# Spreading a tile's row stores over the next tile, and reordering the matmuls, in the backward chain of a recurrent-memory attention block

## The chip, the cores and the metric

The kernel runs on one core of one Trainium2 chip. The metric is device time in microseconds (us) of one execution. Times are medians of several executions; profiles are of one execution each. Runs of one kernel lie 15 to 50 us apart, so where a few microseconds matter I compare stretches inside a trace and not totals.

## The reference

The reference computes a forward pass and all its gradients: layer norm, attention with a recurrent memory, layer norm, a gated FFN. Cut to what matters:

```python
for s in range(n_seg):                       # 64 segments of 32 tokens, one after the other
    h = concat([mem, x[:, 32*s:32*s+32]])    # 8 memory rows + 32 tokens = 40 rows of 448
    q, k, v = h @ Wq, h @ Wk, h @ Wv         # 16 heads of 256
    p = softmax(mask(q @ k.T / 16))
    o = (p @ v) @ Wo
    mem = o[:, :8]                           # goes into the next segment
```

The backward pass runs through the 64 segments in the opposite order. The gradient of `mem` couples each segment to the one before it, so this part cannot be made parallel. I call it the backward chain. A token tile is 128 tokens, that is four segments. `r` is the number of a segment in its tile. The chain runs through r = 3, 2, 1, 0, and the tile's rows are stored when r = 0 is done.

## The kernel before

Forward chain, FFN and weight-gradient tail do not change. In the backward chain, each segment makes row gradients of V, K and Q heads in `blk` (32 token columns per segment) and `lo` (8 memory columns). `blk` and `lo` are stored to HBM once per tile, and the tail reads them. Q, K and V of the forward pass come back by transposing DMA loads in `load_seg`. `k.ps1()` takes one of five PSUM tiles. `k.evac(..., "v")` copies on VectorE (DVE), `"s"` on ScalarE (ACT). `nc.gpsimd.dma_start` is issued by POOL (POOLq in the views) and goes into the software DMA queue (q0 software_dynamic in the profile, 238.56 MB in the whole trace), `nc.sync` is issued by SP (SPq) into a hardware queue (q1 hardware_dynamic, 359.15 MB). `k.prio.crit()` gives the chain priority; the `px` part is filler that the scheduler fits into gaps.

```python
    WoT_sb = W(0, KC, HD)
    WkT_sb, Q_sb = W(32, MC, D), W(60, 16, P)
    WvT_sb, K_sb = W(64, MC, D), W(92, 16, P)
    WqT_sb = W(96, MC, D)
    blk = {nm: A(8 * i, 32, P) for i, nm in enumerate("kqv")}
    lo_b = {nm: [A(24 + 4 * i + 2 * e, 32, 32) for e in range(2)] for i, nm in enumerate("kqv")}
    dxT_b = [A(36 + 2 * e, 1024).bitcast(FP32).rearrange("p (c n) -> p c n", n=P) for e in range(2)]
    om2 = A(40, 1024).bitcast(FP32)
    vT = A(48, 32, 64)
    dO_sb = A(52, 16, P)
    doT = A(56, 32, 64)
    do_roll = A(60, KC, NWIN, L)
    woT_tmp = A(40, HD)
    dhx = A(62.5, KC, P)
    dmr = A(63.5, KC, 16, M)
    P_bd, dS_bd, dST_bd = [B(1.25 * i, 8, 2, L) for i in range(3)]
    Pb = [B(3.75 + 0.625 * i, 8, L) for i in range(2)]
    # ... (cut: prep_tile)
    def load_seg(s):
        nc.sync.dma_start_transpose(out=vT.rearrange("p (a b) n -> p a (b n)", b=2), in_=dr["VG"][s])
        nc.sync.dma_start_transpose(out=Q_sb, in_=dr["QT"][s])
        nc.sync.dma_start_transpose(out=K_sb, in_=dr["KT"][s])
        P_sb = Pb[s % 2]
        nc.gpsimd.dma_start(out=P_sb.rearrange("p h n -> p (h n)"), in_=dr["P_all"][s])
        for g in range(2):
            nc.gpsimd.tensor_copy(out=P_bd[64 * g:64 * g + L, :, g, :], in_=P_sb[64 * g:64 * g + L, :, :])
    # ... (cut: weight loads; then, for segment s from 63 down to 0, t, r = divmod(s, 4):)
            pss = [k.ps1() for _ in range(4)]
            for j in range(MC):
                c = cj(j)
                b, jj = divmod(j, 8)
                for kc in range(KC):
                    nc.tensor.matmul(pss[b][:, jj * L:(jj + 1) * L], lhsT=WoT_sb[:, kc, c * P:(c + 1) * P],
                                     rhs=do_roll[:, kc, sl, :], start=(kc == 0), stop=(kc == KC - 1))
            # ... (cut: evacuation to doT)
            def token_major(hf):
                ph = k.ps1()[:].bitcast(BF16)
                for i in range(8):
                    c0 = 2 * (8 * hf + i)
                    nc.tensor.transpose(ph[:, i * P:(i + 1) * P], doT[:, c0:c0 + 2, :].rearrange("p c n -> p (c n)"), ident[:, :])
                nc.scalar.copy(out=dO_sb[:, 8 * hf:8 * hf + 8, :], in_=ph.rearrange("p (c n) -> p c n", n=P))
            token_major(0)
            pD = k.ps1()
            for h in range(8):
                for g in range(2):
                    for dc in range(DC):
                        j = 2 * (2 * h + dc) + g
                        nc.tensor.matmul(pD[64 * g:64 * g + 64, h * L:(h + 1) * L], lhsT=doT[:, j, :], rhs=vT[:, j, 0:L],
                                         start=(dc == 0), stop=(dc == DC - 1), skip_group_check=True)
            token_major(1)
            # ... (cut: four DVE instructions: prod, rsum, prod, dS_bd)
            pH = k.po1()
            for wi, (nm, lhs, rhs, WT) in enumerate((("v", dO_sb, P_bd, WvT_sb), ("k", Q_sb, dS_bd, WkT_sb),
                                                     ("q", K_sb, dST_bd, WqT_sb))):
                if nm == "k":
                    pT = k.ps1()
                    for h in range(8):
                        for g in range(2):
                            nc.tensor.matmul(pT[64 * g:64 * g + L, h * L:(h + 1) * L], lhsT=dS_bd[:, h, g, :],
                                             rhs=ident[:, 64 * g:64 * g + L], start=True, stop=True, skip_group_check=True)
                    for g in range(2):
                        k.evac(dST_bd[64 * g:64 * g + L, :, g, :],
                               pT[64 * g:64 * g + L, 0:8 * L].rearrange("p (h n) -> p h n", n=L), "vs"[g])
                pp = [k.ps1() for _ in range(3)]
                head_mm(pp, lhs, rhs)
                for b in range(3):
                    c0, n, v = c12(pp[b], b)
                    k.evac(blk[nm][:, c0:c0 + n, r * SEG:(r + 1) * SEG], v[:, :, M:L], "vsv"[b])
                for b in range(3):
                    c0, n, v = c12(pp[b], b)
                    k.evac(lo[nm][:, c0:c0 + n, r * M:(r + 1) * M], v[:, :, 0:M], "svs"[b])
                for j in range(MC):
                    nc.tensor.matmul(pH[32 * (j % 4):32 * (j % 4) + 32, 0:D], lhsT=blk[nm][:, j, r * SEG:(r + 1) * SEG],
                                     rhs=WT[:, cj(j), :], start=(wi == 0 and j < 4), stop=(wi == 2 and j >= MC - 4),
                                     skip_group_check=True)
            nc.vector.tensor_copy(out=om[:, 0:224], in_=pH[:, 0:224])
            nc.scalar.copy(out=om[:, 224:D], in_=pH[:, 224:D])
            # ... (cut: pm = om x sel on TensorE, memory rows of the gradient into do_roll for segment s-1)
            nc.scalar.copy(out=dxT[:, :, r * SEG + M:(r + 1) * SEG], in_=pm3[:, :, 0:24])
        # ... (cut)
        if r == 0:
            for nm in "kqv":
                nc.gpsimd.dma_start(out=dr["X_" + nm][t], in_=blk[nm].rearrange("p c n -> p (c n)"))
                nc.gpsimd.dma_start(out=dr["M_" + nm][t], in_=lo[nm].rearrange("p c n -> p (c n)"))
            px = k.fx1()
            for wi, (nm, WT) in enumerate((("k", WkT_sb), ("q", WqT_sb), ("v", WvT_sb))):
                for j in range(MC):
                    nc.tensor.matmul(px[32 * (j % 4):32 * (j % 4) + 32, 0:D], lhsT=lo[nm][:, j, :], rhs=WT[:, cj(j), :],
                                     start=(wi == 0 and j < 4), stop=(wi == 2 and j >= MC - 4), skip_group_check=True)
            nc.scalar.copy(out=om2[:, 0:D], in_=px[:, 0:D])
            pl = k.fx1()
            for kc in range(KC):
                nc.tensor.matmul(pl[:, kc * 32:(kc + 1) * 32], lhsT=om2[:, kc * P:(kc + 1) * P], rhs=sel[:],
                                 start=True, stop=True)
            nc.scalar.copy(out=dxT.rearrange("p c (r n) -> p c r n", n=SEG)[:, :, :, 0:M],
                           in_=pl[:, 0:KC * 32].rearrange("p (c r m) -> p c r m", c=KC, m=M))
            pX = k.fx1()
            for kc in range(KC):
                nc.tensor.transpose(pX[:, kc * P:(kc + 1) * P], dxT[:, kc, :], k.identf[:, :])
            dxn = k.f32("f3", D, "dxn_sb")
            nc.scalar.copy(out=dxn[:], in_=pX[:, 0:D])
            nc.gpsimd.dma_start(out=dr["DXN"][t * P:(t + 1) * P, :], in_=dxn[:])
```

Of the kernel before, what the change touches and what calls it, by code (L numbers as in the profile page):

```python
# [9 lines left out]
FP32 = mybir.dt.float32  # L10
# [5 lines left out]
P = 128  # L16
# [130 lines left out]
def run_all(k: _K):  # L147
# [18 lines left out]
    k.B = _Arena(arena, "arB", 8.25)  # L166
# [59 lines left out]
def cj(j):  # L226
    return (j % 2) * 16 + j // 2
# [418 lines left out]
def backward_chain(k: _K):  # L646
# [13 lines left out]
    blk = {nm: A(8 * i, 32, P) for i, nm in enumerate("kqv")}  # L660
    lo_b = {nm: [A(24 + 4 * i + 2 * e, 32, 32) for e in range(2)] for i, nm in enumerate("kqv")}
    dxT_b = [A(36 + 2 * e, 1024).bitcast(FP32).rearrange("p (c n) -> p c n", n=P) for e in range(2)]
    om2 = A(40, 1024).bitcast(FP32)
# [4 lines left out]
    woT_tmp = A(40, HD)  # L668
# [13 lines left out]
# [4 lines that stand above are left out]
        P_sb = Pb[s % 2]  # L686
        nc.gpsimd.dma_start(out=P_sb.rearrange("p h n -> p (h n)"), in_=dr["P_all"][s])
        for g in range(2):
            nc.gpsimd.tensor_copy(out=P_bd[64 * g:64 * g + L, :, g, :], in_=P_sb[64 * g:64 * g + L, :, :])
# [5 lines left out]
    nc.gpsimd.memset(do_roll[:, :, (NSEG - 1) % NWIN, SEG:L], 0.0)  # L695
    om = k.f32("f1", DP, "omb")
    nc.gpsimd.memset(om[:], 0.0)
    nc.gpsimd.memset(om2[:, D:DP], 0.0)
# [15 lines left out]
    for s in range(NSEG - 1, -1, -1):  # L714
# [3 lines left out]
        lo = {nm: lo_b[nm][t % 2] for nm in "kqv"}  # L718
        dxT = dxT_b[t % 2]
# [6 lines left out]
        with k.prio.crit():  # L726
# [16 lines left out]
            token_major(0)  # L743
            pD = k.ps1()
# [6 lines left out]
            token_major(1)  # L751
# [9 lines left out]
            for wi, (nm, lhs, rhs, WT) in enumerate((("v", dO_sb, P_bd, WvT_sb), ("k", Q_sb, dS_bd, WkT_sb),  # L761
                                                     ("q", K_sb, dST_bd, WqT_sb))):
                if nm == "k":
                    pT = k.ps1()
                    for h in range(8):
                        for g in range(2):
                            nc.tensor.matmul(pT[64 * g:64 * g + L, h * L:(h + 1) * L], lhsT=dS_bd[:, h, g, :],
                                             rhs=ident[:, 64 * g:64 * g + L], start=True, stop=True, skip_group_check=True)
                    for g in range(2):
                        k.evac(dST_bd[64 * g:64 * g + L, :, g, :],  # L770
                               pT[64 * g:64 * g + L, 0:8 * L].rearrange("p (h n) -> p h n", n=L), "vs"[g])
                pp = [k.ps1() for _ in range(3)]
                head_mm(pp, lhs, rhs)
                for b in range(3):
                    c0, n, v = c12(pp[b], b)
                    k.evac(blk[nm][:, c0:c0 + n, r * SEG:(r + 1) * SEG], v[:, :, M:L], "vsv"[b])
                for b in range(3):
                    c0, n, v = c12(pp[b], b)
                    k.evac(lo[nm][:, c0:c0 + n, r * M:(r + 1) * M], v[:, :, 0:M], "svs"[b])
                for j in range(MC):  # L780
                    nc.tensor.matmul(pH[32 * (j % 4):32 * (j % 4) + 32, 0:D], lhsT=blk[nm][:, j, r * SEG:(r + 1) * SEG],  # L781
                                     rhs=WT[:, cj(j), :], start=(wi == 0 and j < 4), stop=(wi == 2 and j >= MC - 4),
                                     skip_group_check=True)
            nc.vector.tensor_copy(out=om[:, 0:224], in_=pH[:, 0:224])
# [15 lines left out]
        nc.gpsimd.tensor_copy(out=dmr[:, :, jm, :], in_=do_roll[:, :, sl, SEG:L])  # L800
# [4 lines left out]
        if r == 0:  # L805
            for nm in "kqv":
                nc.gpsimd.dma_start(out=dr["X_" + nm][t], in_=blk[nm].rearrange("p c n -> p (c n)"))
                nc.gpsimd.dma_start(out=dr["M_" + nm][t], in_=lo[nm].rearrange("p c n -> p (c n)"))
            px = k.fx1()
            for wi, (nm, WT) in enumerate((("k", WkT_sb), ("q", WqT_sb), ("v", WvT_sb))):  # L810
                for j in range(MC):
                    nc.tensor.matmul(px[32 * (j % 4):32 * (j % 4) + 32, 0:D], lhsT=lo[nm][:, j, :], rhs=WT[:, cj(j), :],  # L812
                                     start=(wi == 0 and j < 4), stop=(wi == 2 and j >= MC - 4), skip_group_check=True)
            nc.scalar.copy(out=om2[:, 0:D], in_=px[:, 0:D])
            pl = k.fx1()
            for kc in range(KC):
                nc.tensor.matmul(pl[:, kc * 32:(kc + 1) * 32], lhsT=om2[:, kc * P:(kc + 1) * P], rhs=sel[:],
                                 start=True, stop=True)
            nc.scalar.copy(out=dxT.rearrange("p c (r n) -> p c r n", n=SEG)[:, :, :, 0:M],
                           in_=pl[:, 0:KC * 32].rearrange("p (c r m) -> p c r m", c=KC, m=M))  # L820
# [5 lines left out]
            nc.gpsimd.dma_start(out=dr["DXN"][t * P:(t + 1) * P, :], in_=dxn[:])  # L826

# [205 lines left out]
```

## Time and profile before

| | |
|---|---|
| median time | 3827.32 us (3823.0 to 3843.95, 3 runs) |
| profiled run | 3806.6 us span |
| backward chain, first segment to last row matmul | 1765.9 to 2967.7 us: 1201.8 us |
| segment length, mean over tiles after the first: r = 3, 2, 1, 0 | 24.31, 16.74, 16.20, 16.62 us |
| shortest and longest r = 3 segment | 19.4 and 33.0 us |

A segment's length is the distance between the first of its 128 output-gradient matmuls (line 732, 128x40) and the first of the next segment's, from the timeline. Segment r = 3 is the first one after a tile's stores were issued. I call it the after-store segment.

The first view is one window over the chain without its first tile. It gives the busy time of each engine with the instructions counted, then the granted TensorE clock, the mean busy share of the 16 DMA engines, and GB/s:

```profile
core 0: us, PE busy (x) PEld busy (x) DVE busy (x) ACT busy (x) POOL busy (x), PEclk, DMA share, GB/s
1862.70:2954.10 1091.40, 943.73 (x21894) 670.66 (x21894) 427.93 (x1062) 390.28 (x990) 164.38 (x389) 0.95 0.79 151
```

TensorE is busy 86% of the time and DMA 79%, so both matter. The second view is the chain of waits, around the start of an after-store segment (start, us, what):

```profile
2316.57 0.48 PE fx L812 x5
2317.05 1.51 PE po L781 x32
2318.57 0.56 PE fx L812 x11
2319.13 0.36 PE psf L788 x2
2319.49 0.02 PE fx L812
2319.51 18.44 DMA arW<-KT
2337.95 0.05 issue
2338.00 0.75 PE psf L711 x16
```

The chain jumps from the Q-head matmuls at 2338.00 back to the DMA that loaded `KT`, and 18.44 us are put down to it. The third view is the DMA issues of the same window (what, issuing queue, how many, KB, median us from issue to landing):

```profile
X_v<-arA POOLq DMA_DIRECT2D x14, 1024.0 KB, 5.9
X_k<-arA POOLq DMA_DIRECT2D x14, 1024.0 KB, 15.5
X_q<-arA POOLq DMA_DIRECT2D x14, 1024.0 KB, 16.0
M_q<-arA POOLq DMA_DIRECT2D x14, 256.0 KB, 16.1
```

X_v, issued first, lands after 5.9 us. X_k and X_q, issued after it, land after 15.5 and 16.0 us.

### The profile page before, as it was taken

How to read it: one execution, taken by the hardware profiler on the slowest of the kernel's cores; microseconds unless marked ns; L12 is line 12 of the kernel's file. 1: busy time of each engine (PE TensorE's matmuls, PEld its weight loads, DVE VectorE, ACT ScalarE, POOL GpSimd, SP SyncE). 2: the span in 40 equal slices, each digit the busy share in tenths (PEclk: the TensorE clock that was granted, in tenths of full speed). 3: DMA queues.
4: the chain of work that ended last, by engine and by line, in shares of the span. 5: the costliest groups of instructions: out<-in, count | busy, mean ns of one | idle time of the engine just before them, and what ended most of it. 6: DMA issues, size and time to landing. Idle time of an engine off the chain costs nothing.

```text
span 3806.6 us, 122548 instructions
## 1 busy us (share of the span) xinstructions
PE 3141.8 (83%) x55484; PEld 2052.6 (54%) x55550; DVE 1350.1 (35%) x2969; ACT 960.6 (25%) x2181; POOL 522.8 (14%) x1129
## 2 busy tenths in 40 slices
PE   3888899888898838892888888889898667888999
PEld 2666666566666625661655656656666333333444
DVE  3443344343343326672333334434443232101101
ACT  1222222222222212330333333333333101111200
POOL 3111111111111111111111111211111111000000
PEclk9999999999998869996999989999999789999999
DMA  7544644545544497789787977787877997777552
GB/s 248 169 155 138 178 148 149 162 148 166 159 149 137 132 192 189 187 198 229 146 135 140 173 128 146 174 143 148 183 142 138 329 193 173 155 154 163 156 191 68
DMA packets 1021838, 629.13 MB, mean 165 GB/s; under 512 B 910148, under 2 KB 940660, under 8 KB 1013572
## 3 DMA queue, kind: packets, MB, share of 16 engines
q1 hardware_dynamic: 934980, 359.15, 46.0%
q0 software_dynamic: 58976, 238.56, 18.4%
q10 hardware_dynamic: 27360, 23.58, 2.2%
q8 instruction: 435, 7.13, 0.8%
q14 instruction: 87, 0.71, 0.1%
HBM read 124.49 MB, written 270.64 MB: 104 GB/s over the span
## 4 chain that ended last, share of the span: by engine, by line
PE 65%; DMA 14%; issue 7%; DVE 5%; SPq 4%; ACT 4%; POOL 1%; ACTq 0%; DVEq 0%; POOLq 0%
PE psf L382 11%; PE po L781 8%; PE psf L905 8%; PE psf L732 5%; PE po L466 4%; DMA arA<-arA 3%; PE psf L711 3%; PE psf L569 2%; PE fx L812 2%; PE psf L423 2%; PE fx L495 2%; PE fx L910 2%; PE fx L363 2%; PE psf L741 2%; PE psf L788 2%
## 5 line engine op out<-in xcount | busy, mean ns | idle before, releaser
L75 DVE CAST arA<-psf 128x320 bf16<-128x320 f32 (+6 forms) x1093 | 500.2, 479 | 1056.3 <-PE psf L905 347.0
L77 ACT CAST arA<-psf 128x480 bf16<-128x480 f32 (+6 forms) x1139 | 440.8, 407 | 1530.5 <-PE psf L382 340.6
L382 PEld LDWEIGHTS <-arW 128*128 128x128 bf16 x16384 | 435.2, 97 | 32.4 <-issue 20.3
L382 PE MATMUL psf<-arA,arW 128*128 128x40 bf16 x16384 | 437.3, 182 | 17.9 <-issue 11.4
L781 PE MATMUL po<-arW,arA 128*32 128x448 bf16 x6144 | 334.2, 360 | 42.5 <-DMA arW<-in_A_Wv_dram 21.2
L732 PE MATMUL psf<-arA,arW 128*128 128x40 bf16 x8192 | 225.7, 182 | 90.2 <-POOL arA L680 39.3
L732 PEld LDWEIGHTS <-arW 128*128 128x128 bf16 x8192 | 223.2, 98 | 107.1 <-issue 102.2
L905 PE MATMUL psf<-arW,arA 128*128 128x512 bf16 x990 | 260.8, 393 | 12.7 <-ACT arA L77 12.7
L905 PEld LDWEIGHTS <-arA 128*128 128x128 bf16 x1440 | 138.7, 100 | 213.6 <-issue 73.4
L781 PEld LDWEIGHTS <-arA 128*32 128x32 bf16 x6144 | 149.2, 97 | 176.4 <-DVE arA L75 44.1
L569 PE MATMUL psf<-arA,arW 128*128 128x256 bf16 x1344 | 166.0, 285 | 72.9 <-DMA arA<-arA 41.1
L569 PEld LDWEIGHTS <-arW 128*128 128x128 bf16 x1344 | 137.2, 102 | 103.8 <-issue 78.4
L75 DVE CAST arB<-psf 40x320 bf16<-40x320 f32 (+2 forms) x256 | 92.4, 361 | 224.8 <-PE psf L457 156.4
L363 PE MATMUL fx<-arW,arA 128*128 128x512 bf16 x456 | 121.7, 388 | 57.9 <-DMA arW<-in_A_Wv_dram 38.6
L926 PE MATMUL psf<-arW 128*128 128x448 bf16 x450 | 105.5, 388 | 62.8 <-DVE arA L75 51.5
L466 PE MATMUL po<-arW,arB 128*8 128x448 bf16 x2048 | 148.1, 445 | 2.9 <-ACT sd L86 0.4
L423 PE MATMUL psf<-arW,arB 128*32 128x512 bf16 x2048 | 149.7, 383 | 0.8 <-issue 0.7
L742 ACT COPY arA<-psf 128x1024 bf16<-128x1024 bf16 x128 | 129.5, 1012 | 55.6 <-PE psf L741 54.0
L457 PE MATMUL psf<-arB,arA 128*128 128x80 bf16 x1024 | 57.9, 221 | 97.3 <-DMA arA<-arA 77.5
L926 PEld LDWEIGHTS <-arW 128*128 128x128 bf16 x606 | 62.5, 104 | 130.2 <-issue 69.4
L812 PE MATMUL fx<-arW,arA 128*32 128x448 bf16 x1536 | 121.8, 368 | 1.5 <-issue 1.5
L495 PE MATMUL fx<-arW,arA 128*128 128x448 bf16 x512 | 120.7, 362 | 0.0
(358 smaller groups left out, 3888.5 us busy)
## 6 DMA issues: line engine op xcount, KB each, us to landing
QT<-arA POOLq DMA_DIRECT2D x64, 512.0 KB, 4.0
KT<-arA SPq DMA_DIRECT2D x64, 512.0 KB
VG<-arA SPq DMA_DIRECT2D x64, 512.0 KB
X_o<-arA POOLq DMA_DIRECT2D x40, 512.0 KB, 4.7
Vx<-arA POOLq DMA_DIRECT2D x32, 512.0 KB, 3.2
arA<-Vx SPq DMA_DIRECT2D x128, 128.0 KB
X_v<-arA POOLq DMA_DIRECT2D x16, 1024.0 KB, 5.9
X_k<-arA POOLq DMA_DIRECT2D x16, 1024.0 KB, 15.5
```

Of the source, the lines that this page charges most:

```text
L75: nc.vector.tensor_copy(out=out, in_=in_)
L77: nc.scalar.copy(out=out, in_=in_)
L363: nc.tensor.matmul(pv[:, 0:512], lhsT=hx_b[t % 2][:, kc, :], rhs=Wv_sb[:, kc, n * 512:(n + 1) * 512], start=(kc == 0), stop=(kc == KC - 1))
L382: nc.tensor.matmul(pss[b][:, jj * L:(jj + 1) * L], lhsT=W_sb[:, kc, c * P:(c + 1) * P], rhs=hT_roll[:, kc, sl, :], start=(kc == 0), stop=( ...
L423: nc.tensor.matmul(pV[b][32 * j:32 * j + 32, 0:512], lhsT=memT_pad[:, kc, :], rhs=Wv_sb[:, kc, n * 512:(n + 1) * 512], start=(kc == 0), st ...
L466: nc.tensor.matmul(pO[32 * (j % 4):32 * (j % 4) + M, 0:D], lhsT=o8[:, j, :], rhs=Wo_sb[:, cj(j), :], start=(j < 4), stop=(j >= MC - 4), sk ...
L495: nc.tensor.matmul(px[:, 0:D], lhsT=xblk[:, j, :], rhs=Wo_sb[:, cj(j), :], start=(j == 0), stop=(j == MC - 1))
L569: nc.tensor.matmul(ps[:, f2 * 256:(f2 + 1) * 256], lhsT=Wt[:, kc, c * P:(c + 1) * P], rhs=xT[:, kc, :], start=(kc == 0), stop=(kc == KC - 1))
L732: nc.tensor.matmul(pss[b][:, jj * L:(jj + 1) * L], lhsT=WoT_sb[:, kc, c * P:(c + 1) * P], rhs=do_roll[:, kc, sl, :], start=(kc == 0), stop ...
L781: nc.tensor.matmul(pH[32 * (j % 4):32 * (j % 4) + 32, 0:D], lhsT=blk[nm][:, j, r * SEG:(r + 1) * SEG], rhs=WT[:, cj(j), :], start=(wi == 0 ...
L812: nc.tensor.matmul(px[32 * (j % 4):32 * (j % 4) + 32, 0:D], lhsT=lo[nm][:, j, :], rhs=WT[:, cj(j), :], start=(wi == 0 and j < 4), stop=(wi ...
L905: nc.tensor.matmul(pa[2 * kc + g][:, 0:w], lhsT=lhs_of(b)[:, kc * P:(kc + 1) * P], rhs=rhs_of(b, g), start=(b == 0), stop=(b == nblk - 1), ...
```

## The change

The intent is threefold. The six stores of a tile (3.75 MB) become nine pieces that are issued over the whole next tile. For that, five row buffers rotate where each of V, K and Q had its own, and `dxT` and the memory columns of Q lose their second buffer to make room. Both transposes of the output gradient come before the score gradients. And the Q-head products are issued inside the K row pass, with the dS transposes after the K heads, so that TensorE has row matmuls to do while other engines evacuate.

```diff
-    blk = {nm: A(8 * i, 32, P) for i, nm in enumerate("kqv")}
-    lo_b = {nm: [A(24 + 4 * i + 2 * e, 32, 32) for e in range(2)] for i, nm in enumerate("kqv")}
-    dxT_b = [A(36 + 2 * e, 1024).bitcast(FP32).rearrange("p (c n) -> p c n", n=P) for e in range(2)]
-    om2 = A(40, 1024).bitcast(FP32)
+    blk_b = [A(8 * i, 32, P) for i in range(5)]
+    lo_b = {"v": [A(40, 32, 32), A(42, 32, 32)], "k": [A(44, 32, 32), A(46, 32, 32)], "q": [B(5, 32, 32)]}
+    dxT = B(7, 1024).bitcast(FP32).rearrange("p (c n) -> p c n", n=P)
     vT = A(48, 32, 64)
     dO_sb = A(52, 16, P)
     doT = A(56, 32, 64)
     do_roll = A(60, KC, NWIN, L)
-    woT_tmp = A(40, HD)
+    woT_tmp = A(24, HD)
 ...
-            nc.gpsimd.tensor_copy(out=P_bd[64 * g:64 * g + L, :, g, :], in_=P_sb[64 * g:64 * g + L, :, :])
+            pool_op = nc.gpsimd.tensor_copy(out=P_bd[64 * g:64 * g + L, :, g, :], in_=P_sb[64 * g:64 * g + L, :, :])
+        stores("mid", s, pool_op.ins)
+
+    pending = {}
+
+    def later(seg, place, fn):
+        pending.setdefault((place, seg), []).append(fn)
+
+    def stores(place, seg, ins):
+
+        for fn in pending.pop((place, seg), []):
+            with tc.issue_after(ins):
+                fn()
 ...
-        lo = {nm: lo_b[nm][t % 2] for nm in "kqv"}
-        dxT = dxT_b[t % 2]
+        tb = NT - 1 - t
+        lo = {nm: lo_b[nm][tb % len(lo_b[nm])] for nm in "kqv"}
+        blk = {nm: blk_b[(3 * tb + i) % 5] for i, nm in enumerate("vkq")}
 ...
             token_major(0)
+            token_major(1)
             pD = k.ps1()
 ...
+            heads("v", dO_sb, P_bd)
+            rows_in("v", WvT_sb, 0, MC)
+            heads("k", Q_sb, dS_bd)
+            pT = k.ps1()
+            for h in range(8):
+                for g in range(2):
+                    nc.tensor.matmul(pT[64 * g:64 * g + L, h * L:(h + 1) * L], lhsT=dS_bd[:, h, g, :],
+                                     rhs=ident[:, 64 * g:64 * g + L], start=True, stop=True, skip_group_check=True)
+            for g in range(2):
+                k.evac(dST_bd[64 * g:64 * g + L, :, g, :],
+                       pT[64 * g:64 * g + L, 0:8 * L].rearrange("p (h n) -> p h n", n=L), "vs"[g])
+            rows_in("k", WkT_sb, 0, 20)
+            heads("q", K_sb, dST_bd)
+            rows_in("k", WkT_sb, 20, MC)
+            rows_in("q", WqT_sb, 0, MC)
 ...
-        nc.gpsimd.tensor_copy(out=dmr[:, :, jm, :], in_=do_roll[:, :, sl, SEG:L])
+        pool_op = nc.gpsimd.tensor_copy(out=dmr[:, :, jm, :], in_=do_roll[:, :, sl, SEG:L])
+        stores("start", s, pool_op.ins)
 ...
-            for nm in "kqv":
-                nc.gpsimd.dma_start(out=dr["X_" + nm][t], in_=blk[nm].rearrange("p c n -> p (c n)"))
+            def store_x(nm, hf, t=t, blk=blk):
+                nc.gpsimd.dma_start(out=dr["X_" + nm][t][:, hf * 2048:(hf + 1) * 2048],
+                                    in_=blk[nm][:, 16 * hf:16 * hf + 16, :].rearrange("p c n -> p (c n)"))
+
+            def store_m(nm, t=t, lo=lo):
                 nc.gpsimd.dma_start(out=dr["M_" + nm][t], in_=lo[nm].rearrange("p c n -> p (c n)"))
+            due = [(lambda: store_x("v", 0), None), (lambda: store_x("v", 1), None), (lambda: store_m("q"), None),
+                   (lambda: store_m("v"), (1, "start")), (lambda: store_m("k"), (1, "start")),
+                   (lambda: store_x("k", 0), (2, "start")), (lambda: store_x("k", 1), (3, "mid")),
+                   (lambda: store_x("q", 0), (3, "start")), (lambda: store_x("q", 1), (4, "mid"))]
+            for fn, at in due:
+                if at is None or s == 0:
+                    fn()
+                else:
+                    later(s - at[0], at[1], fn)
             px = k.fx1()
-            for wi, (nm, WT) in enumerate((("k", WkT_sb), ("q", WqT_sb), ("v", WvT_sb))):
+            for wi, (nm, WT) in enumerate((("q", WqT_sb), ("k", WkT_sb), ("v", WvT_sb))):
 ...
```

In `due`, `None` means at once, and `(n, place)` means in the iteration of the n-th following segment. In the trace the `mid` pieces go out one segment earlier, because the loads that they are tied to run ahead: both halves of X_k leave in the second segment, both of X_q in the third. `tc.issue_after` fixed only their place in POOL's order here.

More of the change, by code (lines that the diff above doesn't have):

```diff
@@ L165, in run_all @@
     k.A = _Arena(arena, "arA", 65)
-    k.B = _Arena(arena, "arB", 8.25)
+    k.B = _Arena(arena, "arB", 9.25)
     k.ps1 = lambda: psum.tile([P, 512], FP32, tag="ps", name="psf", bufs=5)
@@ L695, in backward_chain @@
     nc.gpsimd.memset(do_roll[:, :, (NSEG - 1) % NWIN, SEG:L], 0.0)
+    nc.gpsimd.memset(dxT[:, KC - 1, :], 0.0)
     om = k.f32("f1", DP, "omb")
     nc.gpsimd.memset(om[:], 0.0)
-    nc.gpsimd.memset(om2[:, D:DP], 0.0)
     prep_tile(NT - 1)
@@ L750, in backward_chain @@
                                          start=(dc == 0), stop=(dc == DC - 1), skip_group_check=True)
-            token_major(1)
             pD3 = pD[:, 0:8 * L].rearrange("p (h n) -> p h n", n=L)
@@ L760, in backward_chain @@
             pH = k.po1()
-            for wi, (nm, lhs, rhs, WT) in enumerate((("v", dO_sb, P_bd, WvT_sb), ("k", Q_sb, dS_bd, WkT_sb),
-                                                     ("q", K_sb, dST_bd, WqT_sb))):
-                if nm == "k":
-                    pT = k.ps1()
-                    for h in range(8):
-                        for g in range(2):
-                            nc.tensor.matmul(pT[64 * g:64 * g + L, h * L:(h + 1) * L], lhsT=dS_bd[:, h, g, :],
-                                             rhs=ident[:, 64 * g:64 * g + L], start=True, stop=True, skip_group_check=True)
-                    for g in range(2):
-                        k.evac(dST_bd[64 * g:64 * g + L, :, g, :],
-                               pT[64 * g:64 * g + L, 0:8 * L].rearrange("p (h n) -> p h n", n=L), "vs"[g])
-                pp = [k.ps1() for _ in range(3)]
-                head_mm(pp, lhs, rhs)
+            pps = {}
@@ L774, in backward_chain, with heads @@
+            def heads(nm, lhs, rhs):
+                pps[nm] = [k.ps1() for _ in range(3)]
+                head_mm(pps[nm], lhs, rhs)
                 for b in range(3):
-                    c0, n, v = c12(pp[b], b)
+                    c0, n, v = c12(pps[nm][b], b)
                     k.evac(blk[nm][:, c0:c0 + n, r * SEG:(r + 1) * SEG], v[:, :, M:L], "vsv"[b])
                 for b in range(3):
-                    c0, n, v = c12(pp[b], b)
+                    c0, n, v = c12(pps[nm][b], b)
@@ L779, in backward_chain, with rows_in @@
                     k.evac(lo[nm][:, c0:c0 + n, r * M:(r + 1) * M], v[:, :, 0:M], "svs"[b])
-                for j in range(MC):
+            def rows_in(nm, WT, j0, j1):
+                for j in range(j0, j1):
                     nc.tensor.matmul(pH[32 * (j % 4):32 * (j % 4) + 32, 0:D], lhsT=blk[nm][:, j, r * SEG:(r + 1) * SEG],
-                                     rhs=WT[:, cj(j), :], start=(wi == 0 and j < 4), stop=(wi == 2 and j >= MC - 4),
+                                     rhs=WT[:, cj(j), :], start=(nm == "v" and j < 4), stop=(nm == "q" and j >= MC - 4),
@@ L813, in backward_chain @@
                                      start=(wi == 0 and j < 4), stop=(wi == 2 and j >= MC - 4), skip_group_check=True)
-            nc.scalar.copy(out=om2[:, 0:D], in_=px[:, 0:D])
+            om2 = k.f32("f3", D, "om2")
+            nc.scalar.copy(out=om2[:], in_=px[:, 0:D])
             pl = k.fx1()
             for kc in range(KC):
-                nc.tensor.matmul(pl[:, kc * 32:(kc + 1) * 32], lhsT=om2[:, kc * P:(kc + 1) * P], rhs=sel[:],
+                m = min(P, D - kc * P)
+                nc.tensor.matmul(pl[0:m, kc * 32:(kc + 1) * 32], lhsT=om2[:, kc * P:kc * P + m], rhs=sel[:],
                                  start=True, stop=True)
-            nc.scalar.copy(out=dxT.rearrange("p c (r n) -> p c r n", n=SEG)[:, :, :, 0:M],
-                           in_=pl[:, 0:KC * 32].rearrange("p (c r m) -> p c r m", c=KC, m=M))
+            dx4 = dxT.rearrange("p c (r n) -> p c r n", n=SEG)
+            pl4 = pl[:, 0:KC * 32].rearrange("p (c r m) -> p c r m", c=KC, m=M)
+            nc.scalar.copy(out=dx4[:, 0:3, :, 0:M], in_=pl4[:, 0:3])
+            nc.scalar.copy(out=dx4[0:64, 3, :, 0:M], in_=pl4[0:64, 3])
             pX = k.fx1()
@@ L826, in backward_chain @@
             nc.gpsimd.dma_start(out=dr["DXN"][t * P:(t + 1) * P, :], in_=dxn[:])
+    assert not pending
 def tail_phase(k: _K):
```

## The prediction

> **What bounds the kernel now.** The change touches only the backward chain: about 1766 us (first output-gradient matmul, timeline) to 2974 us of a 3806.6 us span, a recurrence over 64 segments, four to a token tile. By segment starts in the timeline, three of a tile's four segments take 16.0 to 17.2 us, nearly all TensorE chain: the chain of waits from 2359.9 shows 3.35 + 0.45 + 0.62 + 0.57 us of matmuls, 1.16 us waiting for two 1.02 us ACT copies, V rows 1.63, a 1.0 us bubble around the dS transposes, K rows 1.70, a 0.6 us bubble, Q rows 1.73, then 2.04 us to the next segment. The fourth, after a tile's row stores, takes 19.4 to 33.0 us, mean 24.3 over fifteen tiles. The chain shows why: "DMA arW<-KT 18.44" at 2319.5. Six stores (3.75 MB) are issued within 6 us, X_k and X_q land after 15.5 and 16.0 us (DMA view), and issuing that KT transpose takes 12.33 us against 2.81 in a quiet segment. [...]
>
> **What the change does.**
> 1. The same bytes go out in nine pieces over the next tile (about 1.25, 0.5, 1 and 1 MB per segment). DMA records outside the burst give roughly 9 us of transposes and 3.5 us of stores per 16 us: below saturation. Each transpose has some 10 us of slack. I expect the after-store segment to fall from 24.3 to about 16.3 us, fifteen times. Critical.
> 2. Both transposes before the scores: the second ACT copy follows the first directly (-0.15 us), but the dS chain on DVE starts 0.55 us later and, with its new order, ends about 0.7 us later; K heads then wait some 0.3 us.
> 3. Q heads inside K rows, dS transposes after K heads: the 1.0 and 0.6 us bubbles go. Sum of 2 and 3, by hand from these durations: 16.0 to about 15.7 us per segment. Small.
> 4. Cost: dxT is single now, so in the built ACT order the dxT copies of the first two segments come after the third's filler work; their two PSUM tiles stay held, leaving 3 of 5 there, and the built PE order breaks up that segment's V and K heads: estimate 17.4 us. Filler (96 matmuls of 53 ns per tile) has smaller gaps to hide in.
> 5. Start: the last Wo piece moves before the 23 us Wq transpose in the SP order: 0 to -8 us.
>
> Tile estimate: 16.3 + 16.1 + 17.4 + 16.1 + 1 residual DMA wait = 66.9 us against 73.9. Fifteen times 7 = 105 us; start -3. Predicted **3720 us**, 8 in 10 between **3685** and **3762**. Chances: faster by over 2% **0.80**, within **0.19**, slower **0.01**.
>
> **What would show it.** 1: every fourth segment within 1.5 us of the others; the KT/QT wait gone from the chain; X_k, X_q landing in under 8 us. 2, 3: row matmuls wait less on DVE, K heads wait on dS, plain segments 15.5 to 15.9 us. 4: a tile's third segment longest, its dxT copies in a bunch. Forward, FFN and weight-gradient tail unchanged within 10 us.
>
> **What would make it wrong.** Store halves colliding with transposes in every segment; the PSUM hold costing 3 us or more per tile; a lower granted clock in the denser stage; the tail waiting longer for last stores.

A tile of 66.9 us against 73.9, fifteen times 7 us, and 3 us for the start, off the 3827.32 us of the kernel before, make the 3720 us. Two of its inputs, from the trace of the kernel before: in the plain segment from 2359.9 to 2376 us the packets of the hardware queue took 8.4 us (a mean of 16 engines), in the one before it 12.2 us. The `VG`, `QT` and `KT` transposes that were issued from 2347.6 on landed 9.3, 11.3 and 11.1 us before their first matmul. "Below saturation" is an estimate from such numbers.

## The result, and the profile after

| | before | after |
|---|---|---|
| median of the runs at that time | 3825.16 us (3800.02 to 3843.95, 4 runs) | 3676.86 us (3671.49 to 3693.75, 4 runs) |
| profiled run | 3806.6 us | 3670.7 us |
| chain, first segment to last row matmul | 1201.8 us | 1076.9 us |
| segments r = 3, 2, 1, 0 | 24.31, 16.74, 16.20, 16.62 us | 16.74, 16.05, 17.11, 15.98 us |

The ratio of times is 0.9624, with a 95% interval of 0.9559 to 0.9689. A ratio is the mean time of one kernel's fast runs over that of the other's of the same rounds, so it is not quite the ratio of the medians quoted. The forecast of a gain over 2% held. The size did not: 3676.86 us is 8 us below the stated range.

The window over the chain without its first tile, changed kernel:

```profile
core 0: us, PE busy (x) PEld busy (x) DVE busy (x) ACT busy (x) POOL busy (x), PEclk, DMA share, GB/s
1845.10:2817.40 972.30, 930.88 (x21899) 664.47 (x21896) 424.38 (x1062) 385.96 (x1005) 188.24 (x436) 1.00 0.79 170
```

The same matmuls fit into 972.30 us instead of 1091.40, and TensorE is busy 96% of it. The clock rose too, from 0.95 to 1.00; that comes back below.

The chain of waits of the changed kernel, in an after-store segment from its first matmul on (line 744 is the old 732):

```profile
2636.32 3.30 PE psf L744 x128
2639.63 0.97 PE psf L753 x16
2640.60 0.62 PE psf L762 x32
2641.22 0.02 issue
2641.24 0.46 PE psf L722 x8
2641.70 0.49 PE fx L846 x8
2642.19 0.42 PE psf L722 x8
2642.61 1.63 PE po L787 x32
2644.24 0.19 PE fx L846 x4
```

No DMA stands in it. The stores of the changed kernel, in the DMA view:

```profile
X_k<-arA POOLq DMA_DIRECT2D x30, 512.0 KB, 4.0
X_q<-arA POOLq DMA_DIRECT2D x30, 512.0 KB, 3.9
X_v<-arA POOLq DMA_DIRECT2D x28, 512.0 KB, 6.2
M_q<-arB POOLq DMA_DIRECT2D x14, 256.0 KB, 5.5
```

All of this looks like the prediction. But two more views do not fit its reason, the late Q and K transposes. The first is what TensorE's matmuls waited for in the same window of the kernel before (engine, line, what ended the wait: us in total, times, longest):

```profile
PE psf L732 <- issue: 39.2, 8, 12.7
PE psf L749 <- issue: 25.8, 3, 11.6
PE psf L711 <- ACT arA L742: 21.3, 31, 1.0
PE po L781 <- DVE arA L75: 15.0, 44, 0.4
PE psf L741 <- issue: 8.8, 3, 4.6
PE psf L788 <- DVE omb L784: 7.5, 15, 0.5
PE psf L711 <- DMA arW<-QT: 5.7, 2, 4.1
PE psf L711 <- issue: 5.3, 3, 3.2
PE po L781 <- issue: 4.3, 4, 1.9
PE psf L711 <- DMA arW<-KT: 3.9, 2, 3.1
```

The two transposes cost TensorE 5.7 + 3.9 = 9.6 us in all fifteen tiles. The after-store segments are (24.31 - 16.74) x 15 = 114 us too long. The large waits are called "issue", which means that the profile shows nothing that was waited for. The timeline of the kernel before shows how such a wait looks (start, us, engine, line, what, count, idle before and what ended it):

```profile
2241.29 2.84 PE L732 MATMUL psf<-arA,arW 128*128 128x40 bf16 x93 [1.39 <-issue]
2243.97 1.02 PE L741 MATMUL psf<-ident,arA 128*128 128x128 bf16 x8
2244.92 0.94 PE L749 MATMUL psf<-arA 128*64 128x40 bf16 x27
2257.37 0.35 PE L749 MATMUL psf<-arA 128*64 128x40 bf16 x5 [11.52 <-issue]
2257.66 1.03 PE L741 MATMUL psf<-ident,arA 128*128 128x128 bf16 x8
```

TensorE stops for 11.52 us after 27 of 32 like matmuls. The other five read the same two tiles and write the same one, so there is no new data that they could have waited for. I counted TensorE's records (weight loads, matmuls and the semaphore records of its sequencer) from the start of the trace: the pauses at 2241 and 2257 lie 256 records apart, and most others a multiple of 256. Without the semaphore records no more than two of the 24 pauses counted below share a residue modulo 256.

The profile has a DMA queue of the kind "instruction", q8, and all 435 of its packets in the trace are of 16,384 bytes. In the DMA view of the kernel before (window 1862 to 2954; packets, MB, share of 16 engines):

```profile
q8 instruction: 171, 2.80, 1.1%
```

From the first after-store segment to the last row matmul 174 of these packets began, and there are 174 places where the count passes the same residue modulo 256. Of 24 pauses over 1.1 us (from the start of one record to the start of the next), 19 lie exactly there. As many blocks are fetched as TensorE passes such places. So I have a new theory, F: q8 fetches TensorE's instructions, one block for 256 of them, the burst of stores delays these fetches, and TensorE stops for want of instructions. The old one, that late transposes stop it, I call T.

The same list for the changed kernel:

```profile
PE psf L722 <- ACT arA L754: 6.3, 14, 0.5
PE fx L861 <- ACT arB L857: 4.9, 15, 0.3
PE psf L722 <- DVE arB L771: 4.3, 14, 0.3
PE psf L744 <- DVE arA L813: 3.9, 14, 0.3
PE psf L722 <- issue: 3.1, 3, 1.1
PE psf L753 <- issue: 2.8, 1, 2.8
```

Its waits for "issue" are a few microseconds.

### The profile page after: what moved, and what is told of

Read it like the earlier page. It is cut to its first block, busy times and chain, and to the rows that moved or that the text cites. A ratio compares the mean times of both kernels' runs of the same rounds, so it can differ in the third digit from the quotient of the medians.

```text
span 3670.7 us, 122624 instructions
## 1 busy us (share of the span) xinstructions
PE 3122.9 (85%) x55484; PEld 2044.1 (56%) x55550; DVE 1349.2 (37%) x2969; ACT 955.4 (26%) x2197; POOL 547.1 (15%) x1177
## 4 chain that ended last, share of the span: by engine, by line
PE 66%; DMA 12%; DVE 7%; issue 6%; SPq 4%; ACT 4%; POOL 1%; ACTq 0%; DVEq 0%; POOLq 0%
PE psf L382 12%; PE psf L944 8%; PE po L787 6%; PE psf L744 6%; PE po L466 4%; PE psf L722 3%; DMA arA<-arA 3%; PE psf L423 2%; PE fx L846 2%; PE psf L569 2%; PE fx L495 2%; PE fx L949 2%; PE fx L363 2%; PE psf L809 2%; DVE arA L75 2%
## 5 line engine op out<-in xcount | busy, mean ns | idle before, releaser
L75 DVE CAST arA<-psf 128x384 bf16<-128x384 f32 (+6 forms) x1029 | 491.9, 495 | 1002.4 <-PE psf L944 351.2
L77 ACT CAST arA<-psf 128x384 bf16<-128x384 f32 (+6 forms) x1011 | 412.0, 429 | 1475.5 <-PE psf L382 337.1
L382 PEld LDWEIGHTS <-arW 128*128 128x128 bf16 x16384 | 435.4, 98 | 28.9 <-issue 16.8
L382 PE MATMUL psf<-arA,arW 128*128 128x40 bf16 x16384 | 437.5, 182 | 14.6 <-issue 8.0
L787 PE MATMUL po<-arW,arA 128*32 128x448 bf16 x6144 | 346.7, 355 | 21.1 <-DMA arW<-in_A_Wv_dram 21.1
L744 PE MATMUL psf<-arA,arW 128*128 128x40 bf16 x8192 | 217.9, 180 | 46.0 <-POOL arA L679 40.1
L744 PEld LDWEIGHTS <-arW 128*128 128x128 bf16 x8192 | 214.0, 96 | 65.4 <-issue 64.9
L569 PEld LDWEIGHTS <-arW 128*128 128x128 bf16 x1344 | 135.9, 101 | 102.6 <-issue 79.0
L75 DVE CAST arB<-psf 40x320 bf16<-40x320 f32 x320 | 107.4, 336 | 165.1 <-PE psf L457 145.8
L77 ACT CAST arB<-psf 128x96 bf16<-128x96 f32 (+1 forms) x320 | 98.2, 307 | 200.1 <-PE psf L457 100.2
L965 PEld LDWEIGHTS <-arW 128*128 128x128 bf16 x606 | 61.8, 102 | 122.2 <-issue 72.4
L722 PEld LDWEIGHTS <-arW 128*128 128x128 bf16 x2048 | 86.9, 100 | 64.7 <-issue 61.3
```

The source lines that it names most:

```text
L75: nc.vector.tensor_copy(out=out, in_=in_)
L77: nc.scalar.copy(out=out, in_=in_)
L382: nc.tensor.matmul(pss[b][:, jj * L:(jj + 1) * L], lhsT=W_sb[:, kc, c * P:(c + 1) * P], rhs=hT_roll[:, kc, sl, :], start=(kc == 0), stop=( ...
L569: nc.tensor.matmul(ps[:, f2 * 256:(f2 + 1) * 256], lhsT=Wt[:, kc, c * P:(c + 1) * P], rhs=xT[:, kc, :], start=(kc == 0), stop=(kc == KC - 1))
L722: nc.tensor.matmul(ps[b][:, i * 2 * L:(i + 1) * 2 * L], lhsT=lhs[:, cl, :], rhs=rhs_bd[:, cl // 2, :, :].rearrange("p g n -> p (g n)"), st ...
L965: nc.tensor.matmul(pa[i][:, 0:D], lhsT=lhs_of(b, i), rhs=rhs_of(b), start=(b == 0), stop=(b == nblk - 1))
```

## The experiments

The table gives all kernels. "Chain" runs from the first segment to the last row matmul; segment means leave out the first tile; "fetch stalls" are pauses over 0.5 us of TensorE at the block boundary, after the first tile, counted from the packed traces as above (no view prints them), with their number and sum. The kernel before had medians of 3814.83, 3825.15 and 3826.10 us (e1 to e4; e5 to e9; e10 to e13).

| kernel | median us | chain | r = 3 | r = 2 | r = 1 | r = 0 | fetch stalls |
|---|---|---|---|---|---|---|---|
| before | 3825.16 | 1201.8 | 24.31 | 16.74 | 16.20 | 16.62 | 22, 89.9 us |
| e4_before_again | 3829.15 | 1205.7 | 24.60 | 16.76 | 16.14 | 16.71 | 20, 82.5 us |
| after | 3676.86 | 1076.9 | 16.74 | 16.05 | 17.11 | 15.98 | 10, 12.1 us |
| e13_after_again | 3693.09 | 1077.6 | 16.96 | 16.05 | 17.01 | 16.01 | 9, 11.5 us |
| e1_burst | 3775.48 | 1165.9 | 22.66 | 16.08 | 16.90 | 15.99 | 24, 64.6 us |
| e2_order_only | 3777.40 | 1178.1 | 23.56 | 16.05 | 16.42 | 16.30 | 22, 79.9 us |
| e3_stores_only | 3704.57 | 1096.4 | 16.79 | 16.97 | 16.78 | 16.56 | 5, 5.0 us |
| e5_k_at_once | 3792.94 | 1195.1 | 24.63 | 16.07 | 16.93 | 15.98 | 21, 95.3 us |
| e6_scores_first | 3680.38 | 1070.8 | 16.73 | 15.96 | 16.85 | 15.89 | 8, 10.2 us |
| e8_two_dxT | 3682.97 | 1080.9 | 17.28 | 16.06 | 16.54 | 16.21 | 12, 17.6 us |
| e9_dST_first | 3696.02 | 1077.7 | 17.10 | 15.88 | 17.12 | 15.82 | 9, 15.6 us |
| e10_unread (wrong results) | 3874.69 | 1227.8 | 25.41 | 17.17 | 16.29 | 16.78 | 22, 67.3 us |
| e11_act_queue | 3877.73 | 1268.6 | 25.96 | 16.24 | 16.38 | 19.75 | 23, 108.2 us |
| e12_three_fixes | 3662.14 | 1060.3 | 16.86 | 15.81 | 16.42 | 15.82 | 11, 16.6 us |

### e1_burst: all stores at once, everything else as changed

```diff
-                if at is None or s == 0:
+                if True:
```

> The changed kernel with one condition changed: all nine row stores are issued at the end of the tile again, in one burst; five buffers and the new matmul order stay. Theory A (the burst of 3.75 MB delays the Q and K transposes): the after-store segment returns from 16.7 to 20-28 us, other segments stay at 16.0-17.1, total near 3785 us (3760-3810). Rival B (what cost time was that the next tile's evacuations waited for single row buffers to be stored): five buffers cure it whatever the burst, total stays at 3677 +-12 us, after-store segment below 17.5 us.

Measured: 3775.48 us, after-store segment 22.66 us, the others unchanged. Theory A holds as to the burst, and rival B falls as the main cause: with five rotating buffers and the burst, 89 of the 125 us of the chain are lost again (1165.9 against 1076.9). What the buffers and the other parts of the change bring without spreading shows as the 12 us between e2 and this run (1178.1 to 1165.9, one trace each). Which of its effects the burst works through, this run does not say; its stalls lie at the block boundaries like those of the kernel before.

### e2_order_only: the new matmul order alone

```diff
             token_major(0)
+            token_major(1)
             pD = k.ps1()
 ...
-            for wi, (nm, lhs, rhs, WT) in enumerate((("v", dO_sb, P_bd, WvT_sb), ...
+            heads("v", dO_sb, P_bd)
+            rows_in("v", WvT_sb, 0, MC)
+            heads("k", Q_sb, dS_bd)
 ... (as in the change; buffers and stores as before)
```

> The kernel before with only the new matmul order (both transposes before the scores, Q heads inside the K row pass, dS transposes after the K heads); buffers and stores as before. Theory A: the long after-store segment stays (mean 22-26 us), plain segments go from 16.0 to 15.6-15.8, total 3795-3815 us. Rival C (the matmul order brought most of the gain): total below 3745 us.

Measured: 3777.40 us, 18 us less than the lower end that I expected. The chain explains 24 to 28 us of the gain (1178.1 against 1201.8 and 1205.7); the rest is scatter of totals, since the profiled run of this kernel took 3797.3. The after-store segment stayed at 23.56 us. Segments without filler, in the first tile, take 15.7 us, where the kernel before takes 16.0, as summed in the prediction. Rival C falls.

### e3_stores_only: spread stores, old matmul order

```diff
             token_major(0)
-            token_major(1)
             pD = k.ps1()
 ... (token_major(1) after the scores; V, K, Q heads and rows in the old order)
```

> The changed kernel with the old matmul order: spread stores, five buffers, single dxT stay. Theory A: after-store segment below 17.8 us, total 3685-3710 us. Rival C: total above 3750 us.

Measured: 3704.57 us, after-store segment 16.79 us. Theory A holds as to the burst, and rival C falls here too. Going from here to the changed kernel gives the order's share with spread stores: 19 us of chain. Spreading together with its buffers gives 105 to 109 us of chain with the old order (1201.8 and 1205.7 to 1096.4) and 101 us with the new (1178.1 to 1076.9). Spreading alone is the 89 us of e1.

### e4_before_again: the kernel before, a second trace

> The kernel before once more, for a second trace. If the 12 us by which the changed kernel's backward chain started earlier are chance of the run, the end of the FFN matmuls moves here too by several us against the first trace of the same kernel (1726 us), and the distance from there to the first segment stays 39 to 41 us. After-store segments should again scatter between 19 and 34 us, in a different pattern.

Measured: 3829.15 us. The FFN's last matmul came at 1742.9 us in this trace, 1726.2 in the first, and 1713.3 in the changed kernel's. The matmuls come in the same order in both kernels up to there, and the source differs only in the size of one arena. So the 12 us by which the changed kernel's chain began earlier are chance. From there to the first segment it was 37.7 us, a little less than I expected. The after-store segments scattered again, from 20.6 to 29.3 us.

### e5_k_at_once: a burst of 2.25 MB

```diff
-                   (lambda: store_x("k", 0), (2, "start")), (lambda: store_x("k", 1), (3, "mid")),
+                   (lambda: store_x("k", 0), None), (lambda: store_x("k", 1), None),
```

> The changed kernel with the two K row stores moved back to the tile's end: a burst of 2.25 MB instead of 1.25 (changed kernel) or 3.75 MB (e1). If a transpose can be late by a fixed slack of some 10 us before it costs anything, this burst still mostly fits: after-store segment 17-18.5 us, total 3680-3705 us. If each megabyte in the burst costs its share (5.9 us for 2.5 MB between the changed kernel and e1), the segment is 19.1 us and the total about 3715 us.

Measured: 3792.94 us and 24.63 us, above both expectations. In the one trace of each, the segment is even longer than with the full burst of e1 (22.66 us); the totals do not tell the two apart (ratios to before of 0.9908 and 0.9893, intervals 0.9848 to 0.9969 and 0.9832 to 0.9953). This is where T broke: neither a fixed slack nor a price per megabyte lets 2.25 MB cost as much as 3.75. The fetch stalls sum to 95.3 us here. I then sorted 870 fetches of five kernels with a burst (before, its repeat, e1, e2, e5) by what the DMA engines did between the crossing of a block boundary and the start of the next fetch:

| busy share of transposes (hardware queue) and of stores (software queue) meanwhile | fetches | median delay | next boundary stalled over 0.5 us |
|---|---|---|---|
| under 0.15, under 0.1 | 293 | 0.53 us | 0 |
| over 0.6, under 0.1 | 247 | 1.43 us | 2 |
| under 0.15, over 0.4 | 82 | 2.67 us | 34 |
| over 0.6, over 0.4 | 35 | 5.09 us | 23 |

The other 213 fetches lie between these rows. Fetches that began beside both stores and transposes were the latest (5.09 us in the median). Stalls go with the delay: leaving out 25 fetches that cannot be paired surely with a crossing, 1 of 605 that began within 2 us was followed by a stall, and 104 of 174 that began after more than 3 us. In e5 the K stores land late (14.2 us for an X_k half, against 9.3 in e1). That a pairing of stores with transposes makes e5 as dear as it is, is argued from this table, not shown by a run of its own.

### e6_scores_first: scores between the two transposes again

```diff
             token_major(0)
-            token_major(1)
             pD = k.ps1()
 ...
+            token_major(1)
             pD3 = pD[:, 0:8 * L].rearrange("p (h n) -> p h n", n=L)
```

> The changed kernel with the scores back between the two transposes; Q heads stay inside the K rows. By my sums the early transposes gain 0.15 us and lose 0.3 us by the later dS, so undoing them gives plain segments of 15.8-16.0 us and a total 0-10 us lower than the changed kernel's. If the early transposes are a gain as intended, plain segments rise to 16.15 us or more and the total by 10 us or more.

Measured: segments r = 0 of 15.89 us against 15.98, r = 2 of 15.96 against 16.05, and a chain 6 us shorter. My sum for this step was right: this part of the change costs 0.1 us a segment. The total of 3680.38 us does not resolve it.

### e8_two_dxT: a second dxT buffer

```diff
-    dxT = B(7, 1024).bitcast(FP32).rearrange("p (c n) -> p c n", n=P)
+    dxT_b = [B(7 + 2 * e, 1024).bitcast(FP32).rearrange("p (c n) -> p c n", n=P) for e in range(2)]
 ...
+        dxT = dxT_b[t % 2]
 ... (arenas arA 65 to 64.5 KB, arB 9.25 to 11 KB; mask1 in a scratch tile, mh moved to arB)
```

> The changed kernel with two dxT buffers again (2 KB found by moving two small tiles of earlier phases). If the held PSUM tiles lengthen the third segment, it falls from 16.9 to about 16.4 us (what the order-only kernel with two dxT shows), others stay, chain shorter by 6-10 us. If the third segment is long only because the end of the filler falls in it, it stays at 16.8-17.0.

Measured: the third segment fell to 16.54 us in the mean and from 16.91 to 16.43 in the median, as expected if held PSUM tiles lengthen it. The chain did not get shorter (1080.9 us): after-store segments took 17.28 us, with 17.6 us of fetch stalls against 12.1 and 11.5 in the two traces of the changed kernel.

### e9_dST_first: evacuate the dS transposes before K's memory columns

```diff
-            heads("k", Q_sb, dS_bd)
+            heads("k", Q_sb, dS_bd, False)        # without the evacuation of lo
 ... (pT and its two evacuations)
+            lo_out("k")
             rows_in("k", WkT_sb, 0, 20)
```

> The changed kernel, with the evacuation of the memory columns of the K heads put after that of the dS transposes, which Q heads wait for. The trace of the changed kernel shows TensorE idle about 0.3 us before Q heads. If that is on the chain, every segment gets 0.2-0.4 us shorter, total 13-25 us lower (3650-3665). If the time goes to another wait, segments stay within 0.1 us.

Measured: the floor fell by 0.16 us (15.98 to 15.82), less than expected, and the chain not at all (1077.7). The total of 3696.02 us is within the scatter of the changed kernel's two sets of runs.

### e10_unread: transposes that nobody waits for

```diff
     def load_seg(s):
-        nc.sync.dma_start_transpose(out=vT.rearrange(...), in_=dr["VG"][s])
-        nc.sync.dma_start_transpose(out=Q_sb, in_=dr["QT"][s])
-        nc.sync.dma_start_transpose(out=K_sb, in_=dr["KT"][s])
+        if s == NSEG - 1:
+            ... (the three loads as they were)
+        else:
+            nc.vector.tensor_copy(out=pace[:, s, :], in_=dS_bd[:, 0, 0, 0:8])
+            op = nc.sync.dma_start(out=dr["pace"][s], in_=pace[:, s, :])
+            with tc.issue_after(op.ins):
+                nc.sync.dma_start_transpose(out=unread, in_=dr["VG"][s])
+                ... (QT and KT into unread too)
```

> New theory F, from the traces: in the burst TensorE stops at every 256th of its instructions, where a 16 KB block of instructions has to come by DMA and the fetch starts 4 to 5 us late; late Q and K transposes (theory T, my prediction) are few. Test: the kernel before, with the burst, but VG, QT and KT of every later segment are transposed into a tile that nobody reads (wrong results on purpose), paced by a small copy after dS, so that the traffic is there and no matmul can wait for a transpose. T: the after-store segment falls to 17.2 us or less, total near 3715. F: it stays at 21-27 us, stalls at one index modulo 256 sum to 60-100 us over fifteen tiles, total 3790-3830.

The traces behind F, in figures: in the after-store segment at 2321 of the kernel before, the fetches before its two pauses began 4.5 and 4.2 us after the crossing. TensorE did not stop at every boundary: in that whole chain 22 of 174 had a pause over 0.5 us.

Measured: the after-store segment stayed at 25.41 us, with 67.3 us of fetch stalls. T falls as the main cause, F holds. What TensorE's matmuls waited for in this kernel, longest first:

```profile
PE psf L722 <- POOL arB L700: 47.5, 3, 18.7
PE psf L722 <- ACT arA L753: 22.1, 34, 1.0
PE psf L760 <- issue: 20.8, 7, 9.7
PE po L792 <- DVE arA L75: 19.6, 47, 2.4
PE po L792 <- issue: 14.4, 5, 8.8
PE psf L752 <- issue: 12.7, 3, 6.5
```

The first line belongs to the experiment: three times a transposing load of memory rows, once in 16 segments, held POOL's queue up (at 2411 us POOL had stood idle for 30.72 us, until `arA<-arA` landed). Without those three tiles the after-store segment is 22.7 us in the mean of twelve. The total came out above what I expected (3874.69 against 3790 to 3830). In the traces the chain is 26 us longer than in the kernel before (1227.8 against 1201.8), the FFN ended 21 us later (1747.1 against 1726.2), and from the last row matmul to the end it took 25 us more (864.1 against 838.9); I did not follow the last two up.

### e11_act_queue: the same burst by another queue

```diff
-                nc.gpsimd.dma_start(out=dr["X_" + nm][t], in_=blk[nm].rearrange("p c n -> p (c n)"))
-                nc.gpsimd.dma_start(out=dr["M_" + nm][t], in_=lo[nm].rearrange("p c n -> p (c n)"))
+                nc.scalar.dma_start(out=dr["X_" + nm][t], in_=blk[nm].rearrange("p c n -> p (c n)"))
+                nc.scalar.dma_start(out=dr["M_" + nm][t], in_=lo[nm].rearrange("p c n -> p (c n)"))
```

> The kernel before with its six row stores per tile issued by ScalarE (hardware queue) instead of POOL (software queue), still in one burst. If the bytes alone delay the instruction fetches, the after-store segment stays at 22-27 us and the total at 3800-3830. If the software queue does it, the fetch delays in the burst fall below 3 us and the segment below 20 us, total below 3765.

Measured: after-store segment 25.96 us, fetch stalls 108.2 us. The software queue is not the culprit: in the chain q0 (software) moved 8.2 MB here against 66.3 in the kernel before, and q10 (hardware) 55.1 MB. The total is above what I expected; segment r = 0 grew to 19.75 us. In the one that I looked at (2338 to 2351 us) ACT issues the six stores between its evacuations, 0.33 to 0.62 us each. I did not follow that further.

### e12_three_fixes and e13_after_again: a better version, beside the changed kernel

The edit of e12 is that of e6, e8 and e9 together on the changed kernel; e13 is the changed kernel.

> The changed kernel with three edits at once: scores between the transposes (e6), two dxT buffers (e8), dS transposes evacuated first (e9). Segment by segment these gained 0.1, 0.5 per tile and 0.16 us, so a tile's floor should be 64.4 us instead of 65.9 and the chain 15-25 us shorter than the changed kernel's 1077 us; total 3650-3665 against a rerun of the changed kernel. If denser segments are paid back in instruction-fetch stalls, the chain stays at 1065-1080 us and the total within 10 us of the rerun.

> The changed kernel once more, for a second trace and more times. The FFN should end somewhere between 1713 and 1750 us as in the other traces, since nothing before the backward chain differs; chain from first segment to last row matmul 1070-1085 us; total 3675-3695 us.

Measured in the same rounds: e12 3662.14 us (ratio to before 0.9572, interval 0.9527 to 0.9618), e13 3693.09 us (0.9645, interval 0.9605 to 0.9685). The means of their six runs differ by 28 us, though the intervals just overlap. The chain is 17 us shorter (1060.3 against 1077.6). A tile takes 16.86 + 15.81 + 16.42 + 15.82 = 64.9 us against 66.0 in e13 and 65.9 in the first trace, where I expected 64.4. Most of the missing 0.5 us sits in the after-store segments, 16.86 us over a floor of 15.8, with 16.6 us of fetch stalls against 11.5. e12 is faster than the kernel before by 4%, and than the changed kernel by under 1%.

The FFN of e13 ended at 1726.4 us, within the expected span and 13 us later than in the first trace of the same kernel.

## Why the prediction was right or wrong

**Step 1, the size: right. Its reason: wrong.** This is the step of the prediction that failed: the wait that it named. The prediction said of the long segment: "The chain shows why: "DMA arW<-KT 18.44" at 2319.5", and that each transpose has some 10 us of slack. The after-store segment did fall to 16.74 us, where I had 16.3 and 1 us of residual DMA wait. But TensorE did not stand still for those 18.44 us. Inside them, in the timeline, it did a whole segment's work up to the Q heads, interrupted by pauses of 1.11 and 1.95 us at two block boundaries; its own wait for `KT` at the end was 0.87 us:

```profile
2324.37 1.25 PE L732 MATMUL psf<-arA,arW 128*128 128x40 bf16 x44 [1.11 <-issue]
2331.31 2.42 PE L781 MATMUL po<-arW,arA 128*32 128x448 bf16 x24 [1.95 <-issue]
2338.00 0.68 PE L711 MATMUL psf<-arB,arW 128*128 128x80 bf16 x14 [0.87 <-DMA arW<-KT]
```

The chain of waits had jumped over all this, because the last releaser was a DMA issued early. Over fifteen tiles the 114 us are made of 89.9 us of pauses at block boundaries, 11.9 us of other pauses over 1.1 us, and some 12 us that I put down to the clock (a difference, not a measurement). All 22 stalls of the 89.9 us lie in after-store segments. Of the other pauses 10.7 us, counted from start to start, are waits of heads for `QT` and `KT`, so the reason that I gave accounts for about a tenth. e10 shows that the pauses stay when no matmul can wait for a transpose. That they are a want of instructions rests on their place at every 256th record and on the late fetches before them; no run took the fetches themselves away. The remedy was the right one for either reason: from the kernel before to the changed one the fetch stalls fell from 89.9 to 12.1 us, and the matmuls' waits for `QT` and `KT` from 9.6 us to none in the list of waits. That the size came out right on a wrong reason was luck. Only e5 and e10 could tell the two apart.

**The clock.** The granted clock in both traces is 1.0 or 0.5 of full, in records that are multiples of 3.413 us long (all but the last of each trace). The chain of the kernel before, after its first tile, has 116 us at half clock, that of the changed kernel 3.4 us. Of the 116 us, 92 us began within 3.4 us of a pause of over 1 us. Whether such a pause brings the half clock on, and so is paid for twice, no run tests. The other 24 us followed no pause over 0.9 us, and e3, which has hardly any stalls and the old order, still has 37.5 us at half clock, all of it without a pause over 0.9 us before it. Why the clock fell there is not shown. "A lower granted clock in the denser stage", which I feared, was the wrong way round: the denser chain, that of the changed kernel, has the higher clock (1.00 against 0.95).

**Step 2: right.** Early transposes were summed to lose slightly (-0.15 against +0.3 us). e6 shows 0.1 us lost. The waits of K heads on dS that I named appear in the list of waits (L722 on DVE arB L771, 4.3 us).

**Step 3: right.** 15.7 us for a segment without filler, as forecast, in the first tile; 15.98 and 16.05 with filler. The order as a whole is worth 19 to 28 us of chain (e2, e3).

**Step 4: right in kind, a little too dear.** I had 17.4 us for the third segment. It took 17.11 and 17.01 us, and e8 puts 0.5 us of that on the single `dxT`.

**Step 5: right in size, wrong in place.** From the FFN's last matmul to the first segment nothing changed (39.7 before, 40.4 after). But the first tile's first segment fell from 47.4 and 46.2 us to 42.9 and 41.6. It does not come from the matmul order: e2, which has the order alone, took 46.8 us, and every run with the new buffers 41.6 to 44.9 us. This is consistent with weights arriving earlier; no run isolates it.

**The sum.** The error of the number lies in small terms. My tile of 66.9 us was 1.0 us too long, 15 us over fifteen tiles: parts of it are the third segment (0.3), and residual waits of 1 us on top of 16.3 where 0.7 to 0.9 on top of 16.04 were found. The first tile, where I had 3 us for the start and no gain in segments, gained 5.5 us. That makes the chain's -125 of my -105. The earlier FFN end of this trace (13 us) is chance. The rest, 148 us between the medians against 136 between the profiles, is scatter: the kernel before ranged from 3798 to 3851 us, and the rerun of the changed kernel had a median of 3693.09 us, inside my range. My range allowed too little for that scatter of both kernels.

**What stays open.** Why a fetch whose packet takes 1.06 us (median of q8 in the kernel before) starts 4 us late in a burst, or 11 to 16 us late as before the four longest stalls of the kernel before: what it waits for, no run here shows. Why e11's r = 0 segment grew. Why 2.25 MB in e5 cost as much as 3.75 MB in e1. Why the clock fell without a pause.

## What to carry to other kernels

When TensorE pauses in the middle of a run of like matmuls and the profile names nothing that it waited for, count its records, the sequencer's too, and compare them with the packets of the instruction queue. In the kernel before, 19 of 24 pauses over 1.1 us lay a multiple of 256 records apart, at places that the count passes as often as a block of 16,384 bytes was fetched (174), and fetches began 0.53 us after the crossing in quiet stretches but 5.09 us beside stores and transposes (medians, the table in e5). That these pauses are waits for instructions is the best explanation I have, not one that a run isolates. This kernel is fully unrolled, with many small matmuls, and q8 fetched 174 blocks in 1105 us of its chain. Sending its large stores in pieces took the fetch stalls from 64.6 us (e1) to 12.1, though in a plain segment the transposes had landed 9 to 11 us before they were needed. In a kernel like it, that is worth a try. And a long DMA step in the chain of waits is a suspicion, not a finding: look up how long the engine itself stood still for it before building on it (0.87 us here, for a step of 18.44).
